# Rounding of two weight tiles placed later, one product placed earlier, and one difference moved to GpSimd, in a retention and SwiGLU kernel

## The chip, the cores and the metric

The kernel runs on one core of one Trainium2 chip. The metric is the device time of one execution in microseconds (us), lower is better. Executions of the kernel before spread over 1.4 us, so differences well below 1 us are read from traces with care.

## The reference, cut to what matters

```python
# attention: q, k, v of shape (4, 8, 768, 64), float32
state = gamma * state + einsum('bhd,bhe->bhde', k[:, :, t], v[:, :, t])
y[:, :, t] = scale * einsum('bhd,bhde->bhe', q[:, :, t], state)
# x = y as (3072, 512); then the feed-forward block, d_ff = 1536
g = x @ w_gate
out = (g * sigmoid(g) * (x @ w_val)) @ w_out      # the weights come as float64
```

## The kernel before: the parts that matter

The 3072 rows are handled in four segments. The change touches only the first one, from 17 to about 160 us, in which the weights are also read for the first time and made ready. The weights come as pairs of 32-bit words. Each **tile** of gate and value weights (12 of them, tile f for block f) and each of 12 output-weight pieces is rounded to float32 in three steps on three engines. A bank is one of the PSUM buffers into which TensorE's products go, too (`bank` in the traces).

```python
def convert_a(piece, *own):           # ScalarE: absolute value; sign words into PSUM banks
    nc.scalar.activation(d, hi.bitcast(F32), AF.Abs)                      # L241
    for i, o in enumerate(own):
        nc.scalar.copy(banks[o], hi[:, ts(i, 512)].bitcast(F32))          # L244
    nc.scalar.activation(lo.bitcast(F32), lo, AF.Copy, ...)               # L246
def convert_b(piece):                 # VectorE: clamp, shift, then the signs back from PSUM
    nc.vector.tensor_scalar(d, d, ..., op0=ALU.min, op1=ALU.max)          # L252
    nc.vector.tensor_scalar(u, u, 3, None, op0=ALU.logical_shift_left)    # L255
    for i, t in enumerate(signs.pop(piece)):
        nc.vector.scalar_tensor_tensor(v, t, 0x80000000, v, ...)          # L258
def convert_c(piece):                 # GpSimd: adds what the low words round to
    nc.gpsimd.tensor_tensor(d, d, lo, op=ALU.add)                         # L265
    load_next(piece[0])               # the next tile's words into a freed buffer
def sums_t(piece, engine=nc.vector):  # differences of the four quarters of a tile
    sub(both, w[:, ds(B22, 2)], w[:, ds(B12, 2)])                         # L277, T3 and T1
    sub(w[:, T2], w[:, B22], w[:, T1])                                    # L278
    sub(w[:, T4], w[:, B21], w[:, T2])                                    # L279
    if kind == "up":
        keep_wt(a)                    # the finished tile to HBM
```

Each block f multiplies by seven products instead of eight, with differences T of the weights and sums s of x:

```python
def up(f):
    product(x, B11, a_up(0, 0)); nc.scalar.copy(p1, x)      # P1
    if f:
        left[f - 1][0]()              # T4 of the last block, SiLU
    if f + 1 < NF:
        sums_t(("up", f + 1, 0))
    product(wb, T1, s1); nc.scalar.copy(p5, wb)
    for p in at_block[f]:             # one output piece, and tile f + 2
        convert_b(p)
    for p in at_block[f][::-1]:       # tile f + 2 first
        convert_c(p)
    product(x, T2, s2, start=False); nc.scalar.copy(u2, x)
    product(wb, B22, s4, start=False)
    if f:
        left.pop(f - 1)[1]()          # L454, L455: frees the bank that block f + 1 starts in
    tt(hT[:, f, 0], wb, u2, op=add)                                       # L474
    product(x, T3, s3, start=False)
    tt(hT[:, f, 1], x, p5, op=add)                                        # L476
    for i, p in enumerate(at_block[f + 1]):
        convert_a(p, ...)
    product(z, B21, a_up(0, 1)); tt(c11, z, p1, op=add)     # P2, L480
```

The start interleaves steps of the attention (`retain(n)` runs the next n) with the first two tiles. The attention goes through six chunks of 128 time steps, 0 to 5. For each chunk one step makes scores, one the mix (the chunk's output, which ScalarE copies to xT) and one the new state; the sums of x follow every second chunk:

```python
retain(7); convert_a(u0, 0, 1); retain(3); convert_b(u0); convert_c(u0)
retain(3); sums_t(u0)
retain(3)                             # state of chunk 3, sums of x, scores of chunk 5
convert_a(u1, 2, 3)
retain(2)                             # mix and state of chunk 4
convert_b(u1); convert_c(u1)
retain(len(steps))                    # mix and state of chunk 5, last sums of x
convert_a(("down", 0, 0), 4); convert_a(u2, 6, 7)
for f in range(NF - 1):
    up(f)
```

The argument rests on each engine working through its own instructions in the order of this text.

## Time and profile before

| | before |
|---|---|
| median of the runs, us | 746.63 (745.86 to 747.22) |
| span of the profiled run, us | 744.2 |
| PE / DVE / POOL busy, whole span, us | 720.2 / 489.1 / 246.2 |
| sign steps of tiles 1, 2, 11 start (L258), us | 37.81, 48.14, 135.41 |
| period of a middle block, us | 9.66 |

PE is TensorE, DVE VectorE, ACT ScalarE and POOL GpSimd. A timeline line gives the start in us, the length in us, the engine, the source line, the operation, output and inputs, the shape, and in brackets the idle time of the engine before it with what ended it. Half clock is a stretch in which the profile shows a granted TensorE clock of 0.50 (full is 1.00). The lines of the kernel before stand in the prediction below.

### The profile page before, as it was taken

To read this page: it belongs to the slowest core of one execution; us is meant where nothing else is said; L and a number is where in the kernel's file an instruction comes from. 1 tells how busy PE (TensorE), PEld (TensorE's weight loads), DVE (VectorE), ACT (ScalarE), POOL (GpSimd) and SP (SyncE) were. 2 spreads that over 40 slices of the span, in tenths; PEclk is the share of its full clock that TensorE was granted. 3 is DMA by queue.
4 is the path that set the end of the run, shared out by engine and by line. 5 is a ranking of instruction groups with operands and counts; after the bars stand their busy time and mean duration, and the time that the engine had idled before them with its cause. 6 is when DMAs were issued, how large, how long until landed. Compare 5 with 4: busy or idle time off the path is not lost.

```text
span 744.2 us, 11024 instructions
## 1 busy us (share of the span) xinstructions
PE 720.2 (97%) x4196; PEld 625.5 (84%) x4196; DVE 489.1 (66%) x845; ACT 246.7 (33%) x488; POOL 246.2 (33%) x156
## 2 busy tenths in 40 slices
PE   6889999999999999999999999999999999999997
PEld 5745555568888989997888999998888899999886
DVE  2889999997595787877464466757437356567520
ACT  2687777422211333321221224332221133333100
POOL 3533333423100546382210073554310053726000
PEclk9989999999999999999999999999999999999999
DMA  9968886457958667670543256660284155540010
GB/s 318 370 209 261 256 268 212 143 210 250 335 194 337 239 236 260 250 268 29 186 183 128 84 200 207 208 216 29 85 286 144 38 193 203 199 149 1 1 57 29
DMA packets 60821, 139.01 MB, mean 187 GB/s; under 512 B 4576, under 2 KB 27616, under 8 KB 60768
## 3 DMA queue, kind: packets, MB, share of 16 engines
q1 hardware_dynamic: 57312, 132.01, 52.0%
q10 hardware_dynamic: 3456, 6.29, 2.3%
q8 instruction: 33, 0.54, 0.3%
q14 instruction: 20, 0.16, 0.1%
HBM read 101.72 MB, written 36.57 MB: 186 GB/s over the span
## 4 chain that ended last, share of the span: by engine, by line
PE 86%; DVE 6%; issue 3%; ACT 2%; POOL 2%; DMA 1%; ACTq 0%; SPq 0%; DVEq 0%; POOLq 0%
PE bank L550 38%; PE bank L634 25%; PE bank L437 9%; PE bank L643 4%; PE bank L331 3%; PE bank L382 3%; PE bank L378 2%; PE bank L360 2%; POOL ring L265 2%; DVE ring L277 1%; DMA hT<-in_q_t_dram 1%; DVE ring L258 0%; ACT ring L241 0%; DVE xs L420 0%; DVE ring L252 0%
## 5 line engine op out<-in xcount | busy, mean ns | idle before, releaser
L550 PE MATMUL bank<-loadp,ring 128*128 128x192 f32 x720 | 140.6, 327 | 2.8 <-ACT midp L515 2.8
L634 PE MATMUL bank<-wot,hsp 128*128 128x256 f32 x576 | 130.9, 382 | 0.0
L550 PEld LDWEIGHTS bank<-loadp,ring 128*128 128x128 f32 x720 | 120.5, 190 | 4.2 <-ACT midp L515 4.0
L634 PEld LDWEIGHTS bank<-wot,hsp 128*128 128x128 f32 x576 | 107.7, 190 | 15.9 <-issue 0.5
L515 DVE TENSOR_TENSOR iop<-bank,iop 128x384 f32<-128x384 f32 x144 | 79.7, 555 | 56.7 <-PE bank L550 53.6
L550 PE MATMUL bank<-xs,ring 128*128 128x192 f32 x432 | 87.9, 326 | 0.0
L515 POOL TENSOR_TENSOR iop<-hsp,midp 128x768 f32<-128x768 f32 x9 | 16.3, 1816 | 189.3 <-ACT hsp L515 149.4
L585 POOL TENSOR_TENSOR hT<-iop 128x768 f32<-128x768 f32 x36 | 66.5, 1847 | 35.8 <-DVE iop L515 35.8
L515 ACT COPY hsp<-bank 128x384 f32<-128x384 f32 x90 | 42.9, 479 | 99.5 <-PE bank L550 89.8
L550 PEld LDWEIGHTS bank<-xs,ring 128*128 128x128 f32 x432 | 73.2, 190 | 0.0
L437 PE MATMUL bank<-xs,ring 128*128 128x384 f32 x192 | 67.0, 504 | 2.9 <-DVE xs L420 2.9
L550 PE MATMUL bank<-xT,ring 128*128 128x192 f32 x324 | 66.2, 327 | 1.1 <-DVE iop L515 1.1
L634 PE MATMUL bank<-wot,hT 128*128 128x256 f32 x288 | 65.9, 382 | 0.0
L437 PEld LDWEIGHTS bank<-xs,ring 128*128 128x128 f32 x192 | 37.9, 198 | 30.2 <-DVE xs L420 3.5
L634 PEld LDWEIGHTS bank<-wot,hT 128*128 128x128 f32 x288 | 53.8, 190 | 8.2 <-issue 1.4
L515 DVE TENSOR_TENSOR midp<-bank,midp 128x384 f32<-128x384 f32 x72 | 40.0, 555 | 26.3 <-PE bank L550 24.8
L550 PE MATMUL bank<-hsp,ring 128*128 128x192 f32 x288 | 56.8, 327 | 0.0
L550 PEld LDWEIGHTS bank<-xT,ring 128*128 128x128 f32 x324 | 54.8, 190 | 2.3 <-DVE iop L515 2.2
L437 PE MATMUL bank<-xT,ring 128*128 128x384 f32 x144 | 50.6, 491 | 3.2 <-DVE hT L455 3.2
L550 PEld LDWEIGHTS bank<-hsp,ring 128*128 128x128 f32 x288 | 48.4, 190 | 0.5 <-ACT hsp L515 0.5
L437 PEld LDWEIGHTS bank<-xT,ring 128*128 128x128 f32 x144 | 26.5, 190 | 24.4 <-issue 7.8
L385 ACT COPY xT<-bank 128x512 f32<-128x512 f32 x24 | 14.1, 587 | 96.3 <-PE bank L382 96.3
(139 smaller groups left out, 1015.4 us busy)
## 6 DMA issues: line engine op xcount, KB each, us to landing
ring<-unitt SPq DMA_DIRECT2D x50, 896.0 KB, 4.6
unitt<-ring SPq DMA_DIRECT2D x21, 896.0 KB, 4.6
unitb<-ring SPq DMA_DIRECT2D x12, 896.0 KB, 5.9
ring<-unitb SPq DMA_DIRECT2D x21, 512.0 KB, 5.6
out_dram<-iop ACTq DMA_DIRECT2D x24, 256.0 KB, 3.7
loadp<-in_w_val_dram SPq DMA_DIRECT2D x18, 256.0 KB, 5.9
loadp<-in_w_gate_dram SPq DMA_DIRECT2D x9, 512.0 KB, 6.3
midp<-in_w_out_dram SPq DMA_DIRECT2D x12, 256.0 KB, 3.4
```

The costliest lines, as they stand in the source:

```text
L265: nc.gpsimd.tensor_tensor(d.bitcast(I32), d.bitcast(I32), lo.bitcast(I32), op=ALU.add)
L331: nc.tensor.matmul(sp[i][:, ts(n, P)], kt[r, n], qt[r, n], start=True, stop=True, skip_group_check=True)
L360: nc.tensor.matmul(st[:, ts(n, P)], kd[:, ts(n, P)], vn[:, ts(n, P)], start=(n == 0), stop=True, skip_group_check=True)
L378: nc.tensor.matmul(y[:, ts(n, P)], prev[:, n], qd[:, n], start=(n == 0), stop=False, skip_group_check=True)
L382: nc.tensor.matmul(y[ds(D * i, D), ts(n, P)], vn[:, ts(2 * n + i, D)], a[i][:, n], start=(ci == 0 and n == 0), stop=True, skip_group_check ...
L385: nc.scalar.copy(xT[:, :, c // NCK % 2, ts(ci % L, P)], pairs(y))
L437: nc.tensor.matmul(o, w[:, slot, k], a[:, k], start=(start and k == 0), stop=(stop and k == KH - 1), skip_group_check=True)
L515: events.append((t, len(events), lambda: fn(*args, **kw)))
L550: nc.tensor.matmul(o[:, h], w[:, h, slot], rhs, start=(start and h == 0), stop=True, skip_group_check=True)
L585: by_block(9.5, 13.5, lambda r: pool(to[:, r], u2[:, r], p5[:, r], op=add))
L634: nc.tensor.matmul(o, a[:, k], wot[k][:, slot], start=(start and k == 0), stop=(k == FH - 1), skip_group_check=True)
L643: nc.tensor.matmul(o, a_dn(0, 0, u)[:, k], wot[k][:, B11], start=(k == 0), stop=(k == FH - 1), skip_group_check=True)
```

## The change

The intent: TensorE waits 2.88 us for the last sums of x because VectorE rounds tile 1 first, and then runs at half clock. So tile 1 is rounded after the attention is done, P2 of block 0 fills TensorE's time, tile 2 is rounded after block 0's additions, and VectorE is relieved of T4.

```diff
+    def sums_t(piece, engine=nc.vector, last=None):
...
+        if not last:
+            sub(both, w[:, ds(B22, 2)], w[:, ds(B12, 2)], op=ALU.subtract)
+            sub(w[:, T2], w[:, B22], w[:, T1], op=ALU.subtract)
+        if last or kind == "down":
+            sub = last.tensor_tensor if last else sub
+            sub(w[:, T4], w[:, B21], w[:, T2], op=ALU.subtract)
+        if last:
             keep_wt(a)
...  in up(f, between=None):
         product(x, B11, a_up(0, 0))
         nc.scalar.copy(p1, x)
         if f:
             left[f - 1][0]()
-        if f + 1 < NF:
-            sums_t(("up", f + 1, 0))
+            if f + 1 < NF:
+                sums_t(("up", f + 1, 0))
+        else:
+            p2()
         product(wb, T1, s1)
...
-        for p in at_block[f]:
-            convert_b(p)
-        for p in at_block[f][::-1]:
-            convert_c(p)
+        if f:
+            for p in at_block[f]:
+                convert_b(p)
+            for p in at_block[f][::-1]:
+                convert_c(p)
+            if f + 1 < NF:
+                sums_t(("up", f + 1, 0), last=nc.gpsimd)
+        else:
+            sums_t(("up", 1, 0))
+            sums_t(("up", 1, 0), last=nc.gpsimd)
         product(x, T2, s2, start=False)
         nc.scalar.copy(u2, x)
+        if between:
+            between()
...
         tt(hT[:, f, 1], x, p5, op=add)
+        if f == 0:
+            for p in at_block[0]:
+                convert_b(p)
+            for p in at_block[0][::-1]:
+                convert_c(p)
...
-        product(z, B21, a_up(0, 1))
-        tt(c11, z, p1, op=add)
+        if f:
+            p2()
...  the start:
     sums_t(u0)
+    sums_t(u0, last=nc.gpsimd)
     retain(3)
-    convert_a(u1, 2, 3)
-    retain(2)
+    convert_a(u1, 1, 5)
+    retain(len(steps))
     convert_b(u1)
     convert_c(u1)
-    retain(len(steps))
     convert_a(("down", 0, 0), 4)
-    convert_a(u2, 6, 7)
-    for f in range(NF - 1):
+    up(0, lambda: convert_a(u2, 6, 7))
+    for f in range(1, NF - 1):
         up(f)
```

## The prediction

> **What bounds the kernel now.** I read the summary of the profile first, then the windows by stage, then the chain of waits and the timeline of the first 160 us, the only stretch that the diff touches.
>
> ```profile
> PE 720.2 (97%) x4196; PEld 625.5 (84%) x4196; DVE 489.1 (66%) x845; ACT 246.7 (33%) x488; POOL 246.2 (33%) x156
> PEclk9989999999999999999999999999999999999999
> ...
> 40.00:60.00 20.00, 18.04 (x47) 10.41 (x48) 17.50 (x30) 15.66 (x25) 6.15 (x4) 0.83 0.75 229
> 80.00:100.00 20.00, 19.21 (x59) 10.88 (x59) 18.62 (x32) 15.12 (x25) 7.99 (x5) 1.00 0.85 263
> ```
>
> Over the whole span TensorE is the bound (97%). The window lines (after the stretch and its length: busy us of PE, weight loads, DVE, ACT, POOL; clock; DMA share; GB/s) show a different stage in the gate/value blocks (37 to 156 us): DVE is busy 18.62 of 20 us, and from 40 to 60 us the clock averages 0.83. One block in the timeline:
>
> ```profile
> 86.74 1.29 DVE L258 SCALAR_TENSOR_TENSOR ring<-bank,ring 128x512 uint32<-128x512 uint32 x2
> 88.25 2.41 POOL L265 TENSOR_TENSOR ring<-ring,loadp 128x1024 int32<-128x1024 int32 x1 [6.00 <-ACT ring L241]
> 89.10 2.82 PE L437 MATMUL bank<-xT,ring 128*128 128x384 f32 x8 [0.40 <-DVE hT L455]
> 90.62 1.28 POOL L265 TENSOR_TENSOR wot<-wot,midp 128x512 int32<-128x512 int32 x1
> 90.69 1.76 DVE L277 TENSOR_TENSOR ring<-ring 128x512 f32<-128x512 f32 x1 [0.34 <-POOL ring L265]
> 92.48 0.42 DVE L278 TENSOR_TENSOR ring<-ring 128x256 f32<-128x256 f32 x1
> 92.94 0.42 DVE L279 TENSOR_TENSOR ring<-ring 128x256 f32<-128x256 f32 x1
> ```
>
> This is a loop between DVE and POOL: rounding of tile f+2 ends on DVE (L258), POOL adds the low words (L265), DVE makes the differences of that tile (L277 to L279) and then rounds the next. L258 ends at 49.43, 59.01, 68.60, 78.35, 88.03, 97.68: 9.6 to 9.7 us a block from the very first. The "ACT" named as releaser of L265 had been done; DVE's L258 ended 0.2 us before. PE needs less: 28 matmul records a block at 5.16/16 = 0.3225 us (91.76 to 96.92) are 9.03 us, and its 0.4 to 0.5 us wait for L455 makes up the rest. So PE is ahead, and **any time that the DVE chain loses between 25 and 137 us is lost at the end** (from 137.8 us the last two blocks are PE-bound).
>
> The start, where the change acts:
>
> ```profile
> 28.96 1.16 ACT L244 COPY bank<-loadp 128x512 f32<-128x512 f32 x2
> 32.40 0.59 ACT L385 COPY xT<-bank 128x512 f32<-128x512 f32 x1 [1.18 <-PE bank L382]
> 33.39 1.06 PE L378 MATMUL bank<-hsp,state 128*128 128x128 f32 x8
> 34.27 1.29 DVE L337 TENSOR_TENSOR iop<-bank,tab 128x512 f32<-128x512 f32 x2
> 36.35 0.69 DVE L252 TENSOR_SCALAR ring<-ring 128x1024 f32<-128x1024 f32 x1
> 39.88 2.03 DVE L420 TENSOR_TENSOR xs<-xT 128x256 f32<-128x256 f32 x1
> 41.97 8.47 PE L437 MATMUL bank<-xs,ring 128*128 128x384 f32 x16 [2.88 <-DVE xs L420]
> ```
>
> PE waits 2.88 us for the last sums of x, because DVE rounds tile 1 (36.35 to 39.1) first; then its 16 matmuls take 8.47 instead of 5.32 us at half clock. The diff aims at these 6 us.
>
> **The Trainium skill.** "SBUF — State Buffer", section "SBUF: two separate sides": GpSimd and a DVE operation with two SBUF inputs take the shared port pair exclusively, for a whole instruction. The trace agrees: L277 takes 1.76 us beside L265 (its normal 0.68 us appears at 43.08), ending 0.55 us after it; at 39.88 L420 takes 2.03 instead of 0.42. DVE operations that read PSUM run at full speed beside POOL (L455, 0.55 us). "GPSIMD Engine Reference", section "4.1 Engine selection": two-input work is about 2x slower there; the trace has 0.79 us for POOL on 128x256 against DVE's 0.42:
>
> ```profile
> 149.64 0.79 POOL L278 TENSOR_TENSOR wot<-wot 128x256 f32<-128x256 f32 x1
> ```
>
> "TensorE: Matmul & The Clock Gate", section "Part 1: The HAM clock gate": an idle window of about 3.4 us halves the clock, a busy one restores it. The trace has it halved after 3.0 us of idleness, from 41.3 to 48.1 us.
>
> **The change part by part.**
>
> (1) T4 on GpSimd, steady loop. It takes L279 from DVE: 0.46 us between starts. But T4 of tile f+1 stands on POOL after both L265, just where DVE makes L277/L278 of the next tile, and all want the port pair. In the trace at 27.4 to 31.6 us such operations alternate. So: second L265 ends 91.90, L277 runs to 92.45, T4 holds the pair to about 93.2, L278 ends 93.48, next rounding at 93.42, where before it was 93.28. Gain nothing, cost about 0.1 us a block; over seven blocks +0.7.
>
> (2) Sign copies of tile 1 go to banks 1 and 5 instead of 2 and 3. **Bank 5 holds scores of the last chunk**, which DVE reads in the second L337. ACT works in order, so its second L244 (29.5 us before) waits for that L337, and the copy of chunk 4's output (L385, 32.40) waits behind it; bank 7 is the only output bank, so PE's next mix (L378, 33.39) waits too. When is L337? T4 of tile 0 enters POOL at about 30.5, takes 0.79, and pushes the two decay products of the last chunk (1.04 and 1.28) into DVE's x sums, which alternate with them: L367 at 30.45 (1.05 earlier, as L279 is gone), L420 to 32.5, L421 to 34.05, L337 at 34.9 to 36.2. Then ACT: L244 36.3, L246 36.85, L385 37.95 to 38.55; PE's mix at 38.65. PE has been idle since 33.5: 5.1 us, so the clock is halved. At the cold durations of the first 14 us (8 records 2.0 us, 16 records 1.97) mix and state end at 44.65, about when a window restores the clock. DVE idles for 7 us meanwhile: L367 at 44.8 to 45.6, x sums to 47.3.
>
> (3) Rounding of tile 1 moves behind all this: 47.3 to 50.05 instead of 36.35 to 39.1. POOL's add 50.2 to 52.6, L277 52.65, L278 53.3, then the moved L474 and L476 to 54.75, rounding of the first output tile and of tile 2 (4.3 us, as at 44.60 to 48.9) to 59.05. Before, this point was 49.43: **the chain is 9.6 us late.** Next round: POOL to 62.9, L277 ends 63.45, rounding of tile 3 to 68.15 (before 59.01): 9.15 late.
>
> (4) P2 next to P1 gives PE 4 records (1.3 us) before the first product that needs x sums. It covers that wait (B11 and B21 44.7 to 47.3, first sum at 46.0), but moves only work of PE, which isn't the bound.
>
> (5) The load of tile 3 is released by the add of tile 1, at 52.6 instead of 41.6, and lands about 60 (issue to landing 6 us). ACT's conversion of it stands before the first copy of block 1, so PE waits from 56.6 to about 63.8 and may go cold again. DVE doesn't need block 1's results before about 68.5, so I add nothing.
>
> Sum: 9.15 late plus 0.7 for the loop = 9.85; less about 0.4, since L277 does not wait for the port in rounds where PE is late: **+9.4 us, 746.6 + 9.4 = 756.0.** The later stages are PE-bound and only shift.
>
> **Rivals.** (a) The intended gain: T1 starts without the wait and at full clock, 2.88 + 3.15 = 6.0 us, and DVE loses 12 operations of 0.46. For it: both costs stand in the trace. Against it: PE has slack of 0.4 to 0.6 us a block later, so an earlier PE alone gives nothing, and the rounding is itself on the chain. If DVE were not the chain: about 740. (b) Rounding late, but ACT not stopped by bank 5: mix as before, rounding of tile 1 at about 41.1, tile 2 to 52.8, 3.4 us late: about 750. (c) The late load of tile 3 and a second cold period hold DVE too: 2 to 5 us more, 758 to 761.
>
> **Range and chances.** Executions of before spread over 1.4 us. My L337 is uncertain by 0.7, the phase of the clock windows by 2, the loop by 1, the load by 3; rival (b) sets the low end, (c) the high end: 748 to 762. Two per cent is 14.9 us: faster needs 731.7, which even (a) doesn't reach; slower needs 761.5. Chances: faster 0.01, same 0.89, slower 0.10.
>
> **What would show it right or wrong.** Right: ACT's L244 into the second bank right after L337 at about 36; PE idle some 5 us before the last mix, then half clock; L258 of tile 2 ending near 59; blocks of 9.6 to 9.8 us; everything after 160 us shifted by one constant. Wrong: L385 of chunk 4 still near 32.4 (step 2 falls), block periods near 9.1 (step 1 falls, the gain would be 4 us), or PE without waits from block 3 on (then DVE isn't the chain).

## More of the kernel before

Line numbers move a little in other versions of the kernel: in the changed one L258 and L265 stay, the differences L277 and L278 are L280 and L281, and T4 (L279) is L284. In e6 the sign steps are L262, GpSimd's additions L273 and the first difference L285.

## The result, and the profile after

The changed kernel takes 754.13 us (753.29 to 755.05, five runs) against 746.63: slower by 7.5 us, which is within the 2% that the prediction calls same. The ratio is 1.0101, with a 95% interval of 1.0088 to 1.0115.

The page and the windows of the changed kernel answer to the first lines of the prediction (in a window line, after its length: busy us of PE, weight loads, DVE, ACT and POOL, then clock, DMA share and GB/s):

```profile
PE 720.2 (96%) x4196; PEld 626.1 (83%) x4196; DVE 486.7 (65%) x833; ACT 246.3 (33%) x488; POOL 259.0 (34%) x168
...
40.00:60.00 20.00, 15.30 (x61) 9.06 (x60) 11.81 (x23) 10.86 (x20) 4.97 (x3) 0.93 0.35 110
80.00:100.00 20.00, 19.73 (x62) 11.36 (x61) 18.69 (x29) 15.23 (x27) 10.36 (x8) 1.00 0.81 252
```

TensorE has the same work (720.2 us). From 40 to 60 us VectorE is busy 11.81 us where it was 17.50. In the middle blocks it is as full as before (18.69 us), although twelve of its instructions are gone.

The timeline at the start, where the time went:

```profile
34.73 1.29 DVE L342 TENSOR_TENSOR iop<-bank,tab 128x512 f32<-128x512 f32 x2
36.05 0.61 ACT L244 COPY bank<-loadp 128x512 f32<-128x512 f32 x1 [6.33 <-DVE iop L342]
37.60 0.57 ACT L390 COPY xT<-bank 128x512 f32<-128x512 f32 x1
38.31 1.87 PE L383 MATMUL bank<-hsp,state 128*128 128x128 f32 x8 [4.70 <-ACT xT L390]
39.37 0.85 DVE L372 TENSOR_TENSOR state<-state,bank 64x256 f32<-64x256 f32 x2 [3.35 <-ACT state L361]
43.91 0.85 DVE L372 TENSOR_TENSOR state<-state,bank 64x256 f32<-64x256 f32 x2 [3.68 <-ACT state L361]
46.39 0.69 DVE L252 TENSOR_SCALAR ring<-ring 128x1024 f32<-128x1024 f32 x1
```

Read the brackets from top to bottom. ScalarE's second sign copy waits 6.33 us for VectorE's L342, which reads the scores in bank 5. Only then comes the copy of chunk 4's output (37.60, before at 32.40), and only then TensorE's last mix, after 4.70 us of idleness. VectorE, the engine of the loop, idles twice, 3.35 and 3.68 us, for ScalarE's scaled states. Rounding of tile 1 starts at 46.39 instead of 36.35.

A middle block of the changed kernel:

```profile
84.98 1.29 DVE L258 SCALAR_TENSOR_TENSOR ring<-bank,ring 128x512 uint32<-128x512 uint32 x2
86.49 2.42 POOL L265 TENSOR_TENSOR ring<-ring,loadp 128x1024 int32<-128x1024 int32 x1 [4.82 <-PE bank L442]
88.86 1.30 POOL L265 TENSOR_TENSOR wot<-wot,ring 128x512 int32<-128x512 int32 x1
88.94 1.77 DVE L280 TENSOR_TENSOR ring<-ring 128x512 f32<-128x512 f32 x1 [0.35 <-POOL ring L265]
90.11 1.19 POOL L284 TENSOR_TENSOR ring<-ring 128x256 f32<-128x256 f32 x1
90.75 0.83 DVE L281 TENSOR_TENSOR ring<-ring 128x256 f32<-128x256 f32 x1
91.50 0.41 DVE L252 TENSOR_SCALAR wot<-wot 128x512 f32<-128x512 f32 x1
```

T4 (L284) and VectorE's L280 and L281 take turns: L281 takes 0.83 us where L278 took 0.42. From the start of the differences to the next rounding it is 91.50 - 88.94 = 2.56 us; before it was 93.28 - 90.69 = 2.59. VectorE lost one operation and the time stayed. In block 0, beside VectorE operations that read PSUM, T4 takes 0.72 us and not 1.19:

```profile
52.99 0.72 POOL L284 TENSOR_TENSOR ring<-ring 128x256 f32<-128x256 f32 x1 [1.33 <-DVE ring L281]
```

There is one more wait, the most striking of the trace, in block 1:

```profile
58.92 1.12 ACT L241 ACTIVATE ring<-loadp 128x1024 f32<-128x1024 f32 x1 [2.32 <-DMA loadp<-in_w_gate_dram]
62.58 5.73 PE L442 MATMUL bank<-xs,ring 128*128 128x384 f32 x12 [5.90 <-ACT iop L467]
```

TensorE waits 5.90 us for a ScalarE copy that stands behind the conversion of tile 3, which waits for a late load. Whether this wait costs anything is one of the questions for the experiments.

To compare the runs I use one mark: when the sign steps of a tile start on VectorE. Tile 0 shows how far the unchanged beginning differs between profiles. Each row is one profiled run; the ratio is from the timed runs, each to the runs of before of the same rounds (medians of those in the later series: 746.03 to 746.09).

| kernel | tile 0 | tile 1 | tile 2 | tile 3 | tile 11 | median us | ratio |
|---|---|---|---|---|---|---|---|
| before | 23.61 | 37.81 | 48.14 | 57.72 | 135.41 | 746.63 | 1 |
| after | 23.77 | 47.84 | 56.74 | 65.82 | 142.98 | 754.13 | 1.0101 |
| e1, ScalarE's order | 24.12 | 43.70 | 52.59 | 61.67 | 138.84 | 749.53 | 1.0044 |
| e2, after with T4 on VectorE | 23.84 | 47.60 | 56.96 | 66.50 | 144.65 | 755.11 | 1.0121 |
| e3, before with T4 on GpSimd | 24.38 | 39.38 | 48.83 | 58.35 | 135.49 | 745.25 | 0.9986 |
| e5, after with tile 3 loaded early | 23.50 | 47.54 | 56.43 | 65.52 | 142.62 | 753.67 | 1.0100 |
| e4, before with P2 next to P1 | 24.82 | 39.03 | 49.93 | 59.51 | 136.77 | 747.22 | 1.0012 |
| e8, after with rounding back | 23.90 | 38.40 | 51.53 | 60.63 | 137.74 | 748.03 | 1.0026 |
| e6, before with split rounding | 23.52 | 37.74 | 47.38 | 55.56 | 127.30 | 739.87 | 0.9916 |
| e7, combined | 23.66 | 40.49 | 49.52 | 57.67 | 130.39 | 742.33 | 0.9944 |
| e9, combined, tile 3 later | 24.21 | 42.54 | 51.58 | 59.73 | 131.87 | 741.62 | 0.9934 |

For the changed kernel the mark adds up: tile 1 is 10.03 us late; from tile 1 to 2 it wins 1.43 back (8.90 instead of 10.33); from tile 2 to 11 another 1.03 (86.24 instead of 87.27). 10.03 - 1.43 - 1.03 = 7.57 us, which is the 7.5 us of the result (0.16 of it is there at tile 0 already). After this stage nothing changes: ScalarE's copies to xT come 7.3 us later throughout, from 176 to 569 us.

### The profile page after: what moved, and what is told of

Same layout as the page of the kernel before. It is cut to its first block, busy times and chain, and to the rows that moved or that the text cites. A ratio compares the mean times of both kernels' runs of the same rounds, so it can differ in the third digit from the quotient of the medians.

```text
span 751.5 us, 11038 instructions
## 1 busy us (share of the span) xinstructions
PE 720.2 (96%) x4196; PEld 626.1 (83%) x4196; DVE 486.7 (65%) x833; ACT 246.3 (33%) x488; POOL 259.0 (34%) x168
## 4 chain that ended last, share of the span: by engine, by line
PE 81%; DVE 7%; issue 4%; DMA 3%; POOL 3%; ACT 2%; ACTq 0%; SPq 0%; DVEq 0%; POOLq 0%
PE bank L574 38%; PE bank L658 24%; PE bank L442 5%; PE bank L667 4%; PE bank L387 3%; PE bank L336 3%; POOL ring L265 3%; PE bank L383 2%; PE bank L365 2%; DVE ring L280 1%; DMA hT<-in_q_t_dram 1%; DMA loadp<-in_w_gate_dram 1%; DMA hT<-in_k_t_dram 1%; DMA tab<-in_decays_dram 1%; POOL ring L284 0%
```

## The experiments

My theory was that of the prediction: VectorE and GpSimd form the loop that sets this stage, and the change makes the loop late at its start, above all by stopping ScalarE on bank 5. The rivals: T4 on GpSimd costs the time; or the late load of tile 3, through which the changed kernel's chain of waits runs, costs it.

**e1: only ScalarE's place.** The sign banks stay; the conversion moves behind chunk 4's steps.

```diff
+    retain(2)
     convert_a(u1, 1, 5)
     retain(len(steps))
```

> The changed kernel, with ScalarE's conversion of tile 1 placed two steps later in program order (after the mix and the state of chunk 4), banks 1 and 5 kept. My theory (ScalarE, in order, is stopped by bank 5 and stops the mix, and the DVE chain is late by that): the copy of chunk 4's output is back near 32.4 us, the last mix near 35 to 37 instead of 38.3 to 42.1, the clock stays full, rounding of tile 1 starts near 42 instead of 46.4, and the whole gains about 4.3 us: 749.8 us. Rival, T4 on GpSimd costs the time: no gain, 754. Rival, the late load of tile 3 sets the path: it comes about 4 us earlier too, so this run doesn't separate it from mine; the fourth run does.

```profile
32.89 0.59 ACT L390 COPY xT<-bank 128x512 f32<-128x512 f32 x1 [4.31 <-PE bank L387]
34.48 1.16 PE L383 MATMUL bank<-hsp,state 128*128 128x128 f32 x8 [0.55 <-POOL hsp L351]
42.25 0.69 DVE L252 TENSOR_SCALAR ring<-ring 128x1024 f32<-128x1024 f32 x1
58.56 3.96 PE L442 MATMUL bank<-xs,ring 128*128 128x384 f32 x6 [6.02 <-ACT iop L467]
```

The copy is back at 32.89, the mix at 34.48 at full speed, rounding starts at 42.25, and the kernel takes 749.53 us: ratio 1.0044 instead of 1.0101, so 0.57% of 746, or 4.3 us, were ScalarE's stop. Note the last line: TensorE's wait in block 1 is even longer here (6.02 us) while the whole is faster.

**e2 and e3: only T4.** e2 is the changed kernel with T4 back on VectorE, e3 the kernel before with T4 on GpSimd.

```diff
 e2, in sums_t of the changed kernel:
-        if last or kind == "down":
-            sub = last.tensor_tensor if last else sub
-            sub(w[:, T4], ...)
-        if last:
-            keep_wt(a)
+            sub(w[:, T4], ...)
+            if kind == "up":
+                keep_wt(a)
 e3, in the kernel before (sums_t as in the change):
     sums_t(u0)
+    sums_t(u0, last=nc.gpsimd)
...
             convert_c(p)
+        if f + 1 < NF:
+            sums_t(("up", f + 1, 0), last=nc.gpsimd)
```

> The changed kernel with T4 of all gate/value tiles back on VectorE, at its old place; all else as changed. My theory: GpSimd's T4 takes from the port pair what VectorE is relieved of, so the block period stays 9.6 to 9.7 us (9.61 changed, 9.66 before) and the time within 0.6 us of the changed kernel: 754.5. Rival, T4 on GpSimd costs the 7.5 us: about 747. Rival, T4 on GpSimd is a real relief of the chain: about 758.

> The kernel before with only T4 of the gate/value tiles moved to GpSimd, at the places the change gives it. My theory: a wash, 746.2 us (period 9.61 instead of 9.66 over seven blocks is 0.4 us). Rival, it costs: 748 to 753. Rival, it is a real relief of 0.46 us a block: 741 to 743.

e2 takes 755.11 us, ratio 1.0121; e3 745.25, ratio 0.9986 with an interval of 0.9972 to 1.0000. Both point to a gain of about 1 us in all from T4 on GpSimd: 1.0121 - 1.0101 is 1.5 us, 1 - 0.9986 is 1.0 us. The timed runs alone don't settle its size (e2's interval, 1.0107 to 1.0135, overlaps the changed kernel's), but the traces agree with it. From tile 2 to 11 it is 87.69 against 86.24 in e2 and after, and 87.27 against 86.66 in before and e3. In the middle blocks the gain is 0.05 us (periods of 9.61 and 9.66); in the changed kernel 0.46 comes in one round, tile 2 to 3 (9.08 us, in e2 9.54), where no T4 lies beside VectorE's differences. So the rival that T4 costs the time falls, and so does the hope that it is a relief of 0.46 us a block. The sign of my own small term was wrong too, and e2's 1.5 us lies outside the 0.6 that I had allowed.

**e5: only the late load.** Tiles 3 and 4 swap their raw buffers; tile 3's is then free earlier.

```diff
-    loadp[:, ds(0, 2048)], loadp[:, ds(2048, 2048)], hsp[:, ds(0, 2048)]]
+    loadp[:, ds(0, 2048)], hsp[:, ds(0, 2048)], loadp[:, ds(2048, 2048)]]
```

> The changed kernel with the raw words of tile 3 loaded into a buffer that is free at about 40 us instead of 51.7 (tiles 3 and 4 swap their raw buffers). ScalarE's conversion of tile 3 then starts near 56.6 instead of 58.9, TensorE's wait of 5.9 us in block 1 shrinks to about 3.5. My theory (the loop of VectorE and GpSimd is the path, TensorE catches up): no change, 754.0 within 0.5. Rival (the chain of waits of the changed kernel goes through this load, 6.2 us of DMA): 2.3 us or more faster, 748 to 752.

```profile
59.84 6.98 PE L442 MATMUL bank<-xs,ring 128*128 128x384 f32 x12 [3.45 <-ACT iop L467]
```

TensorE's wait falls from 5.90 to 3.45 us, as expected, and the ratio is 1.0100 where it was 1.0101. So these 2.45 us of the wait cost nothing. The changed kernel's trace shows why: after its wait TensorE runs from 65.3 to 96.7 us without another one and catches up, while VectorE's sign steps stay 9.54 to 9.62 us apart; then it waits for VectorE again:

```profile
96.97 2.82 PE L442 MATMUL bank<-xT,ring 128*128 128x384 f32 x8 [0.27 <-DVE hT L460]
```

**e4: only P2.** The kernel before with P2 of block 0 next to P1 (`p2` as in the change).

```diff
         product(x, B11, a_up(0, 0))
         nc.scalar.copy(p1, x)
+        if f == 0:
+            p2()
...
+        if f:
+            p2()
-        product(z, B21, a_up(0, 1))
-        tt(c11, z, p1, op=add)
```

> The kernel before with only the first block's P2 moved next to P1. My theory (TensorE is ahead of the chain, so earlier work of it gives nothing): its wait of 2.88 us before the first product of sums shrinks to about 1.6, the clock probably stays full, yet the time is the same, 745.9 within 0.6, and the wait returns later as more wait for VectorE in blocks 1 to 4. Rival (the intent): 3 to 6 us faster, 740 to 743.

```profile
43.20 1.56 PE L437 MATMUL bank<-xs,ring 128*128 128x384 f32 x4 [1.27 <-DVE xs L420]
44.97 0.56 DVE L459 TENSOR_TENSOR iop<-bank,iop 128x384 f32<-128x384 f32 x1 [0.57 <-ACT iop L462]
```

The wait for the sums shrinks to 1.27 us, the clock stays at 1.00, so TensorE is some 2.5 us earlier (an estimate from the two traces: block 1's first product ends at 50.4 us instead of about 52.9), and the kernel takes 747.22 us, ratio 1.0012 (1.0000 to 1.0024). The intended gain is not there, as expected, and the time won comes back as waits of TensorE for VectorE (1.78 us at 52.20, 1.61 at 61.87). That it is slightly slower I had not expected. Part of it is visible: the addition that goes with P2 (L459) now stands ahead of tile 1's differences on VectorE and waits 0.57 us for ScalarE, and from tile 1 to 2 it takes 10.90 instead of 10.33 us. By tile 11 most of this is made up (the 1.36 us of the table contain 1.21 from before tile 0, where the program is unchanged), so the 0.9 us of the timed runs are not explained in full.

**e8: only the rounding of tile 1 back.** The changed kernel, with tile 1 in its old place and banks.

```diff
-    convert_a(u1, 1, 5)
-    retain(len(steps))
+    convert_a(u1, 2, 3)
+    retain(2)
     convert_b(u1)
     convert_c(u1)
+    retain(len(steps))
```

> The changed kernel with the rounding of tile 1 back where it was before (between the state of chunk 4 and the last mix, sign banks 2 and 3); T4 on GpSimd, P2 next to P1 and the order inside block 0 as changed. My theory: most of the loss goes, what stays is that rounding of tile 2 waits behind two sums that need the second-last product of block 0 (about 2 us), less what T4 gave (0.8): 747.0 within 1.5. Rival (the order inside block 0 costs as much as the start): 750 or more.

```profile
46.79 0.56 DVE L493 TENSOR_TENSOR hT<-bank,iop 128x384 f32<-128x384 f32 x1 [1.39 <-PE bank L442]
48.02 0.56 DVE L495 TENSOR_TENSOR hT<-bank,iop 128x384 f32<-128x384 f32 x1 [0.68 <-PE bank L442]
```

748.03 us, ratio 1.0026: of the 1.01% only 0.26% stay. The two lines show what stays: VectorE now waits 1.39 and 0.68 us for TensorE before it may round tile 2; from tile 1 to 2 it takes 13.13 instead of 10.33 us, 2.8 more, less the 1.06 that T4 gives from tile 2 to 11 (86.21). So of the changed kernel's loss, 1.0101 - 1.0026, or 5.6 us, stands for the place of tile 1's rounding with its banks, of which e1 gave back 4.3.

**e6: the loop itself.** If the loop is the bound, its longest avoidable wait is L277's 1.76 us beside GpSimd's second addition. In the kernel before, e6 splits the rounding: the SBUF steps of both pieces first, then the sign steps of both, and GpSimd adds the output piece first.

```diff
         for p in at_block[f]:
-            convert_b(p)
-        for p in at_block[f][::-1]:
+            convert_b1(p)             # clamp and shift
+        for p in at_block[f]:
+            convert_b2(p)             # signs, from PSUM
+        for p in at_block[f]:
             convert_c(p)
```

> The kernel before with one thing changed in every block: VectorE first does the two SBUF steps of the rounding of both pieces (output tile, then gate/value tile), then the sign steps of both, which read PSUM; and GpSimd adds the low words of the output tile first. GpSimd's add of the output tile then lies beside VectorE's sign steps and not beside its differences. My theory (the loop is the bound and the port pair makes its longest wait): the differences take 0.7 instead of 1.76 us, the loop falls from 9.66 to about 8.5 us, TensorE with 9.03 us becomes the bound, and some 5 us go: 741.0. Rival (the loop isn't what sets the stage): no change, 746.

```profile
82.15 1.28 DVE L262 SCALAR_TENSOR_TENSOR ring<-bank,ring 128x512 uint32<-128x512 uint32 x2
82.38 1.30 POOL L273 TENSOR_TENSOR wot<-wot,midp 128x512 int32<-128x512 int32 x1 [5.33 <-DVE wot L262]
83.65 2.42 POOL L273 TENSOR_TENSOR ring<-ring,loadp 128x1024 int32<-128x1024 int32 x1
86.47 0.56 DVE L490 TENSOR_TENSOR iop<-bank,iop 128x384 f32<-128x384 f32 x1 [0.73 <-PE bank L445]
86.94 0.68 DVE L285 TENSOR_TENSOR ring<-ring 128x512 f32<-128x512 f32 x1
```

GpSimd's addition of the output piece now lies beside the sign steps, which keep their 1.28 us; the differences take 0.68 us. VectorE waits for TensorE (0.73), no longer the other way round. The sign steps of the middle blocks are 9.03 us apart (73.12, 82.15, 91.18), TensorE's own pace, and the kernel takes 739.87 us, ratio 0.9916: 6.3 us faster than before. That the DVE-POOL loop set the stage is thereby shown from the other side.

**e7 and e9: can the intended gain be had then?** With TensorE the bound, its earlier start should count. e7 joins the split with P2 next to P1, T4 on VectorE, tile 3 loaded early, and this start:

```diff
-    convert_a(u1, 1, 5)
-    retain(len(steps))
-    convert_b(u1)
+    retain(2)
+    convert_a(u1, 1, 4)
+    convert_b1(u1)
+    retain(1)                         # mix of chunk 5
+    steps.reverse()                   # the last sums of x before its state
+    retain(2)
+    convert_b2(u1)
     convert_c(u1)
-    convert_a(("down", 0, 0), 4)
+    convert_a(("down", 0, 0), 5)
```

> The split order of rounding (as the run before), T4 on VectorE, P2 next to P1, and the start put so that nothing is late: ScalarE's conversion of tile 1 after chunk 4's steps (sign banks 1 and 4), the last sums of x between the SBUF steps and the sign steps of tile 1, the raw words of tile 3 loaded early. With TensorE the bound of the stage, the intended gain should now be real: first sums ready near 38.5 us, no half clock, block 0 ends some 9 us earlier than before, a wait of about 2 us for ScalarE in block 1: 738 within 3. If TensorE's earlier start is worth nothing even then: 741, as the split alone.

```profile
40.26 5.32 PE L448 MATMUL bank<-xs,ring 128*128 128x384 f32 x16
...
52.93 1.61 PE L448 MATMUL bank<-xs,ring 128*128 128x384 f32 x4 [3.14 <-ACT iop L473]
55.52 5.49 PE L448 MATMUL bank<-xs,ring 128*128 128x384 f32 x8 [0.98 <-ACT iop L481]
```

The start is as planned: the products of sums begin at 40.26 at full clock. But block 1 gives it back: waits of 3.14 and 0.98 us for ScalarE, behind tile 3's conversion, and then eight records in 5.49 us at half clock. It takes 742.33 us, slower than the split alone, a miss. In the changed kernel such a wait was free. Here the sign steps from tile 4 on are 9.03 us apart, TensorE's own pace, so nothing is made up; but e7 differs from e6 in several things, and its time alone names no cause. e9 moves the conversion of tile 3 behind block 1's first copies:

```diff
+        if f == 1:
+            convert_a(("up", 3, 0), 6, 7)     # and not at the end of block 0
         if f:
             for p in at_block[f]:
                 convert_b1(p)
```

> The combined kernel with one move: ScalarE's conversion of tile 3 (3.2 us) no longer stands before block 1's first copies (P1, the two SiLU, P5) but after them. In the combined kernel TensorE waited 3.14 and 0.98 us there and then ran 8 matmul records in 5.5 instead of 2.6 us at half clock, which is 7 us of the 9 that its start had won. My theory (with TensorE the bound, every wait of it counts): the wait becomes one of about 2.7 us before the last product of sums, without half clock; 738 within 1.5, so 4 us faster than the combined kernel. Rival (something else ate the gain): 742.

```profile
56.66 1.56 PE L448 MATMUL bank<-xs,ring 128*128 128x384 f32 x4 [1.95 <-ACT iop L497]
62.08 4.41 PE L448 MATMUL bank<-xT,ring 128*128 128x384 f32 x8 [2.58 <-DVE hT L466]
```

741.62 us (739.90 to 743.82), a miss too: the wait only moved, 1.95 us to a later copy and 2.58 us to VectorE, and there is half clock again (61.9 to 65.3 us). The profiled run is the slowest of the six and 0.6 us late at tile 0. What these two runs leave open is whether any start beats that of e6; I did not find one. e6 is the fastest kernel by its ratio (0.9902 to 0.9929, which overlaps e9's 0.9921 to 0.9946).

## Why the prediction was right, point by point

- **The bound.** Right. The loop of VectorE and GpSimd sets the stage: e4 and e5 change TensorE's waits without gain, and e6 shortens the loop and gains 6.3 us.
- **Bank 5 stops ScalarE, and that TensorE and VectorE.** Right, step by step in the trace: L244 at 36.05 (predicted 36.3), the copy at 37.60 (37.95), the mix at 38.31 (38.65). e1 measures it alone: 4.3 us.
- **Mix and state end at 44.65.** Too late by 1.5 us: they end at 43.15. The clock was full again at 41.9 us, 3.4 us after it was halved at 38.5, and not at about 44.65, so the state took 1.16 instead of 2.0 us. This is most of why tile 2's sign steps start at 56.74 and not at the 57.76 that follow from the prediction (59.05 less their 1.29).
- **T4 on GpSimd costs 0.1 us a block.** This term of the sum was wrong, by sign. The mechanism, taking turns at the port pair, stands in the trace. The size didn't: T4 ended 0.59 us after L280 (91.30 less 90.71), where I had put 0.75, from a line of 0.79 us that begins while a VectorE difference still runs. The stretch became 2.56 us, not 2.73. From tile 2 to 3 the changed kernel wins 0.50 us, as my times had it (9.6 late, then 9.15). From tile 3 to 11 it wins another 0.53 (77.16 us against 77.69), where I had booked a net cost of 0.3 (0.7 less 0.4). The 0.4, for a difference that doesn't wait for the port while TensorE is late, is not seen where TensorE is latest: L280 at 60.57 took 1.77 us.
- **The late load of tile 3 adds nothing.** Right, by e5. TensorE's second cold period, which I had named as possible, came (half clock from 59.0 to 65.8 us) and was hidden too: TensorE had caught up by 96.97 us. This is also why one of my signs of being wrong, TensorE without waits from block 3 on, came true for a while although VectorE was the chain.
- **The sum.** 9.4 predicted, 7.5 measured: about 1.0 from the earlier clock at the start (tile 2 is 8.60 us late, not 9.6), about 0.8 from T4 and the loop after tile 3 (0.53 won, 0.3 booked as a cost). Both errors made the prediction too high.
- **Rivals.** (a), the intended gain, falls: TensorE's earlier work was worth nothing as long as it wasn't the bound. (b), late rounding without the stop, is what e1 ran: predicted about 750, measured 749.53. That the number fits so well is partly luck: tile 2 was 4.45 us late there (0.5 of it already at tile 0) and not 3.4, and from tile 2 to 11 e1 won 1.02 back. (c) falls by e5.

## What to carry to other kernels

Before work is moved to relieve a waiting engine, ask which engine sets the pace of the stage over many blocks: here the wait that was to be removed lay on an engine with slack, and the move delayed the loop that had none. When a scratch buffer is exchanged, ask who still reads the new one and what stands behind the writer in its engine's order; one copy into a busy bank cost 4.3 us through two other engines. And where two engines share a port, moving an operation from one to the other need not relieve either (T4: 0.05 us a block); placing the one's SBUF work beside the other's PSUM work did.

## What the Trainium skill lacked or had wrong

- "SBUF — State Buffer", section "SBUF: two separate sides", gives the lock for a whole instruction. It doesn't say how two full queues share it: here they take turns, instruction by instruction. T4 takes 0.72 us alone and 1.19 in the loop; L281 takes 0.42 alone and 0.83.
- "TensorE: Matmul & The Clock Gate", section "Part 1: The HAM clock gate", tells of an idle window of about 3.4 us. Here shorter waits had half clock with them: in the kernel before one of 2.88 us (41.3 to 48.1 us; it began 2.2 us after the last matmul ended at 39.1 by the trace, not after the 3.0 us that the prediction reads), in e9 one of 2.58 us. A wait of 1.27 us in e4 had none. The ends of matmuls are modelled in these traces.
- "GPSIMD Engine Reference", section "4.1 Engine selection", gives about 2x for two-input work. The 128x256 difference took 0.72 us on POOL against 0.42 on DVE, which is 1.7x.
